# Taking the last head's K pass out of a loop and loading its second half in smaller pieces, in a one-core attention-decode kernel

## Chip, cores, metric

One Trainium2 chip, one of its cores. The metric is device time in microseconds (us) of one execution. The kernel before took 1300.07 us (median of 4 executions, 1299.55 to 1300.87). The profile is of a further execution, of 1300.63 us; its span, which leaves out start and end, is about 1.8 us shorter than the time.

## The reference

A decode step for one token: layer norm, 32-head attention over a cache of 32,768 positions per head, output projection, residual, layer norm, a small MLP, residual.

```python
h = x + A(layernorm(x))           # x: 1 x 1 x 512, bf16
#   q = (x @ wq) as 32 heads of 128
#   p = softmax(q . k_cache * 128**-0.5)     k_cache: 32 x 32768 x 128 bf16
#   A = (p @ v_cache) as one row @ wo        v_cache: the same shape
out = h + B(layernorm(h))         # 512 -> 1376 -> 512, h * tanh(softplus(h))
```

The two caches are 8 MB per head each, 512 MB in all, read once. Everything else is small.

## The kernel before

PE is the engine for matmuls, DVE the vector engine, ACT the scalar engine; SBUF is the memory on the chip, PSUM the memory that matmuls write. K and V of a head stand in SBUF in one ring of two halves of 8 MB. A head is 32 groups of 8 x 128 positions. For each group PE transposes K (8 matmuls against an identity), DVE copies the result from PSUM, PE forms the scores (8 matmuls), and, 40 groups behind, PE forms the values of the head before (8 matmuls). A load is 4 MB, half a head, and is issued when the half that it overwrites has been used. The last V has no half of its own: it goes where the last K was, as soon as that is transposed.

The plan of the loads (cut):

```python
PIECE = 128
FIRST = [8, 8, 16, 32, 64, 128]          # K of head 0
LAST = [128, 64, 32, 16, 8, 8]           # V of head 31
LAG = 8
...
for h in range(H):
    for kind in "kv":
        own = h == 0 if kind == "k" else h == H - 1
        sizes = (FIRST if kind == "k" else LAST) if own else [PIECE] * NH      # NH = 2
        ...
        if kind == "k":
            after = [f"trb{(h - 1) * GH + g1 - 1}"] if h else []     # K: after the same groups of the K before
        else:
            after = [f"pv{(h - 1) * GH + g1 - 1}"] if h else ...     # V: after the values of the V before
            if own:
                after = [f"trb{h * GH + g1 - 1}"]                    # V 31: after the transposes of K 31
```

128 in such a list is 4 MB in rows of 32 KB per partition; 64 has 16 KB rows, 32 has 8 KB rows, and so on.

Only PE's program has a loop. DVE, ACT and the queue of loads are straight code; PE runs heads 2 to 31 as 30 rounds of one body:

```python
for hk in range(2):
    for t in range(GH):
        group(hk, t)

S.repeat(range(2, H), whole)              # whole(hk): the 32 groups of head hk

for t in range(GH):                       # after the last K: values alone
    group(H, t)                           # t = 1: maximum of the last scores, t = 3, 4: to all partitions, exp
    if t == 1:
        y_init()
        for h in range(H - 2, H):
            w_bar(h)                      # row sums on DVE
        ...
    if 2 <= t <= LAG:
        ... y_cols(h) ...                 # 4 "column products" per head, 30 heads: wo times the head's output
```

After that come the column products of the last head, a layer norm, the MLP and the store.

Of the kernel before, what the change touches and what calls it, by code (L numbers as in the profile page):

```python
# [13 lines left out]
PE, ACT, DVE, POOL, SP = "pe", "act", "dve", "pool", "sp"  # L14


PIECE = 128
FIRST = [8, 8, 16, 32, 64, 128]
LAST = [128, 64, 32, 16, 8, 8]

LAG = 8

# [138 lines left out]
def plan_loads(H, GH):  # L161


    NH = GH * 8 // PIECE
    loads = []
    for h in range(H):
        for kind in "kv":
            own = h == 0 if kind == "k" else h == H - 1
            sizes = (FIRST if kind == "k" else LAST) if own else [PIECE] * NH
            assert sum(sizes) == GH * 8 and max(sizes) <= PIECE  # L170
            g = 0
            for j, n in enumerate(sizes):
                g1 = g + n // 8
                if kind == "k":
                    after = [f"trb{(h - 1) * GH + g1 - 1}"] if h else []
                    pos, count = h * GH + g, h
                else:
                    after = [f"pv{(h - 1) * GH + g1 - 1}"] if h else ["q_done"] if g1 > GH // 2 else []
                    if own:
                        after = [f"trb{h * GH + g1 - 1}"]  # L180
                    pos, count = (h + 1) * GH + LAG + g + 0.5, h + 1
                chan = f"{kind}own{j}" if own else f"{kind}{j}"
                loads.append(_Load(kind, h, g, g1, pos, chan, 16 if own else 16 * count, after))
                g = g1
    loads.sort(key=lambda x: x.pos)
    return loads


def build_kernel(nc, A_x, A_k_cache, A_v_cache, A_wq, A_wo, B_w1, B_b1, B_w2, out, NE=4):
# [3 lines left out]
    H = HD // Dh  # L193
# [5 lines left out]
    GH = Sk // (128 * R)  # L199
    NCOL = GH * R  # L200
    NK = H * GH
    FJ = (F + 127) // 128
# [28 lines left out]
    identb = sb([128, 128], BF16, "identb")  # L231
# [25 lines left out]
    FP = FJ + FJ % 2  # L257
    b1r = sb([FP, 128], BF16, "b1r")
    b1T = sb([128, FJ], F32, "b1T")
# [8 lines left out]
    hlp = ps([128, 512], "hlp")  # L268
    yps = ps([128, 512], "yps")
    T_b = [ps([128, R * 128], f"tps{i}", BF16) for i in range(2)]  # L270
# [3 lines left out]
    M_REG = hlp[:, 132:132 + KC]  # L274
    V_REG = hlp[:, 140:141]
    Q0 = 160
    YC = yps[:, 0:KC * WIDE:WIDE]
    HROW = 128
    YM = yps[:, 256:257]
# [32 lines left out]
    def program(S):  # L312
        t_ = nc.tensor
        a = nc.scalar
        v = nc.vector
# [4 lines left out]
        def issue(ld):  # L320
            cache = A_k_cache if ld.kind == "k" else A_v_cache

            part, n = divmod(ld.g0 * R, PIECE)
            src = cache[0, ld.h, part * PIECE * 128:(part + 1) * PIECE * 128, :].rearrange(
# [27 lines left out]
        for _, ld in sorted(order, key=lambda o: o[0]):  # L352
            if isinstance(ld, str):
                load_weights(ld)
            else:
                issue(ld)
        S.dma(SP, lambda: sp.dma_start(out[0, 0, :].rearrange("(g n) -> g n", g=4), outsb[0:128:32, :]).then_inc(sems["out"], 16),
              waits=["fin"])
# [29 lines left out]
               name="ident", waits=["iota"])  # L388
# [20 lines left out]
        def transposes(i):  # L409
            ld = kload.get(i)  # L410
            tb = T_b[i % 2]
            hk, t = i // GH, i % GH
            waits, take = ["identb"] if hk == 0 else [], {}
            if ld:
                waits.append((ld.chan, ld.count))
                if hk:
                    take[1] = (ld.chan, 16)
            if hk >= 2 and t in (GH // 4, 3 * GH // 4):
                half = 1 if t == GH // 4 else 0
                take[2] = (f"{DVE}{half}{PRIV}", DVE_ROUND[half])  # L420
            if hk >= 2 and t == GH // 2 + 4:
                take[3] = (ACT + PRIV, 2)
            if i >= 2:
                waits.append(f"ev{i - 2}")
            for r in range(R):
                S.step(PE, lambda r=r: t_.matmul(  # L426
                    tb[:, r * 128:(r + 1) * 128], block("k", i, r), identb[:, :],
                    is_transpose=True, start=True, stop=True),
                    name=(f"trb{i}" if r == R - 1 else None), waits=(waits if r == 0 else ()), take=take.get(r))
# [22 lines left out]
        def values(i):  # L452
            h, g = divmod(i, GH)
            ld = vload.get(i)
            ob = o_b[0 if g < GH - LAG else 1]
            waits, take = [], {}
            if g == 0:
                waits.append(f"exp{h}")
            if g == GH - LAG:
                waits.append(f"exq{h}")  # L460
            if ld:
                waits.append((ld.chan, ld.count))
                if h < H - 1:
                    take[1] = (ld.chan, 16)
            for r in range(R):
                c = g * R + r
                S.step(PE, lambda r=r, c=c: t_.matmul(  # L467
                    ob[:, 0:WIDE], block("v", i, r), pbuf[:, c:c + 1].to_broadcast([128, WIDE]),
                    start=(r == 0 and g in (0, GH - LAG)), stop=(r == R - 1 and g in (GH - LAG - 1, GH - 1))),
                    name=(f"pv{i}" if r == R - 1 else None), waits=(waits if r == 0 else ()), take=take.get(r))  # L470

        def y_cols(h):
            waits = [f"oT{h}", ("wo", 16)]
            for c in range(KC):
                S.step(PE, lambda c=c: t_.matmul(  # L475
                    yps[:, c * WIDE:(c + 1) * WIDE], wo_sb[:, h, c * 128:(c + 1) * 128],
                    oT[:, h:h + 1].to_broadcast([128, WIDE]),
                    start=False, stop=(h == H - 1), skip_group_check=True), waits=(waits if c == 0 else ()),
                    name=(f"yc{h}" if c == KC - 1 else None))
# [12 lines left out]
        def group(hk, t):  # L492
# [49 lines left out]
            if 0 <= iv < NK:  # L542
                values(iv)
# [15 lines left out]
        def w_bar(h):  # L559
            S.step(DVE, lambda: v.tensor_reduce(wbar[:, h:h + 1], wo_sb[:, h, :], AXX, ALU.add), waits=[("wo", 16)],  # L560
                   name=f"wbar{h}")
# [6 lines left out]
            for t in range(GH):  # L568
                group(hk, t)

        S.repeat(range(2, H), whole)


        hl = H - 1
        for t in range(GH):
            group(H, t)
            if t == 1:
                y_init()
                for h in range(H - 2, H):
                    w_bar(h)  # L580
                S.step(DVE, lambda: v.tensor_scalar_mul(wbh[:, 0:1], wbar[:, hl:hl + 1], 1.0 / D), name="wbh0",
                       waits=[f"wbar{hl}"])
                S.step(DVE, lambda: v.scalar_tensor_tensor(
                    wbh[:, 1:2], wbar[:, hl:hl + 1], 1.0 / D, wbh[:, 0:1], ALU.mult, ALU.subtract), name="wbh",
                    waits=["wbh0"])
            if 2 <= t <= LAG:
                for h in range((H - 2) * (t - 2) // (LAG - 1), (H - 2) * (t - 1) // (LAG - 1)):
                    y_cols(h)
            if t == LAG + 2:
                y_cols(H - 2)  # L590
                S.step(DVE, lambda: v.tensor_tensor(wbo[:, 0:hl], wbar[:, 0:hl], oT[:, 0:hl], ALU.mult), name="wbo",
                       waits=[f"yc{H - 2}"])
                S.step(DVE, lambda: v.tensor_reduce(wbs[:, :], wbo[:, 0:hl], AXX, ALU.add), name="wbs", waits=["wbo"])
            if t == LAG + 6:
                S.step(PE, lambda: t_.matmul(YM, onesm[:, :], wbs[:, :], start=False, stop=False, skip_group_check=True),
                       waits=["wbs"])
                S.step(PE, lambda: t_.matmul(T_b[0][:, 0:FP], b1r[:, :], identb[0:FP, 0:FP],
                                             is_transpose=True, start=True, stop=True),
                       name="b1t", waits=[("b1", 32), f"ev{NK - 2}", f"ev{NK - 1}"])
                S.step(DVE, lambda: v.tensor_copy(b1T[:, :], T_b[0][:, 0:FJ]), name="b1T", waits=["b1t"])  # L600
        for t in range(LAG):
            group(H + 1, t)

# [3 lines left out]
        for s in range(2):  # L607
            S.step(PE, lambda s=s: t_.matmul(
                YM, wbh[:, s:s + 1].to_broadcast([128, 128]), oT[:, hl:hl + 1],
                start=False, stop=(s == 1), skip_group_check=True),  # L610
                waits=(["wbh"] if s == 0 else ()), name=("ym" if s == 1 else None))
        S.step(DVE, lambda: v.tensor_scalar(HC, YC, YM, MEANX, ALU.subtract, ALU.subtract),
               name="hc", waits=["ym"])
# [4 lines left out]
        for j in range(FJ):  # L618
            W = 128 if j < FJ - 1 else FLAST
            for kc in range(KC):  # L620
                S.step(PE, lambda j=j, W=W, kc=kc: t_.matmul(  # L621
                    pre[0:W, j:j + 1], w1v[:, kc, j * 128:j * 128 + W], xcT[:, kc:kc + 1],
                    start=(kc == 0), stop=(kc == KC - 1)),
                    name=("hid" if j == FJ - 1 and kc == KC - 1 else None),
                    waits=(["xcT", ("w1", 16), f"exq{H - 1}"] if j == 0 and kc == 0 else ()))
            if j == FJ // 2:
                S.step(PE, lambda: t_.matmul(V_REG, onesm[:, :], SSQ2, start=True, stop=True), name="v2",
                       waits=["ssq2"])
        S.step(ACT, lambda: a.activation(LNV2, V_REG, ACTF.Ln, bias=EPSC), name="ln2", waits=["v2"])
        S.step(ACT, lambda: a.activation(RSTD2, LNV2, ACTF.Exp, scale=-0.5), name="rstd2", waits=["ln2"])  # L630
        for c in range(KC):
            S.step(PE, lambda c=c: t_.matmul(
                yps[32 * c:32 * c + 1, HROW:HROW + 128], hcol[:, c:c + 1], ident[:, :],
                start=False, stop=False, skip_group_check=True), waits=(["hcol"] if c == 0 else ()))
        z, zm, e, u, uz, den, rden = (hs[:, k, :] for k in range(7))
        S.step(DVE, lambda: v.scalar_tensor_tensor(z, pre[:, 0:FJ], RSTD2, b1T[:, :], ALU.mult, ALU.add),
               name="z", waits=["hid", "rstd2", "b1T"])
# [7 lines left out]
        for j in range(FJ):  # L645
            W = 128 if j < FJ - 1 else FLAST
            waits = ["act", ("w2", 32)] if j == 0 else ()
            for c in range(KC):
                S.step(PE, lambda j=j, W=W, c=c: t_.matmul(  # L649
                    yps[32 * c:32 * c + 1, HROW:HROW + 128], actT[0:W, j:j + 1], w2v[0:W, j, c * 128:(c + 1) * 128],  # L650
                    start=False, stop=(j == FJ - 1), skip_group_check=True),
                    name=("y2" if j == FJ - 1 and c == KC - 1 else None), waits=(waits if c == 0 else ()))
# [46 lines left out]
```

## Time and profile before

| stage | us from the span's start | read from |
|---|---|---|
| first half of K 31 lands, PE starts it | 1238.9 | chain of waits |
| PE has done its 16 groups | 1255.5 | timeline |
| second half of K 31 lands, PE starts it | 1259.3 | timeline |
| PE leaves the loop | 1275.1 | timeline |
| exp of the last scores | 1279.4 | timeline |
| last values done | 1290.6 | chain |
| end of span | 1298.8 | page |

First the page: DMA busy in tenths and GB/s in 40 slices of the span, and the DMA queues with number of packets, MB and share.

```profile
span 1298.8 us, 52290 instructions
...
DMA  9999999999999999999999999999999999999994
GB/s 375 423 411 409 431 430 431 434 433 430 429 434 433 430 430 433 430 432 432 433 429 432 433 431 431 431 434 429 426 431 429 432 432 429 432 432 430 431 433 184
...
q1 hardware_dynamic: 26840, 548.09, 98.8%
q8 instruction: 21, 0.34, 0.1%
q14 instruction: 13, 0.11, 0.0%
```

The loads run at about 430 GB/s to the last slice, so the body is bound by them. The Trainium skill, "DMA: Bandwidth & Descriptors", "Specifications", gives a fabric ceiling of 435 GB/s; the slices agree. Queues 8 and 14 are not data: they bring the engines' instructions. On queue 8 a packet is 16 KB; on queue 14 one is 8 KB.

Next the timeline of PE around the gap: start, length, engine, line, what it did, and in brackets the idle time before it and what ended it. In the names of the program `tps` are the transposes of K, `sps` the scores, `ops` the values and `yps` the column products.

```profile
1255.13 0.35 PE L467 MATMUL ops<-pbuf,ring 128*128 128x32 bf16 x8
1259.29 1.03 PE L426 MATMUL tps<-identb,ring 128*128 128x128 bf16 x8 [3.81 <-DMA ring<-in_A_k_cache_dram]
...
1260.60 1.01 PE L426 MATMUL tps<-identb,ring 128*128 128x128 bf16 x8
```

PE sits idle for 3.81 us until the second half of K 31 lands. Then eight transposes take 1.0 us instead of 0.6: the clock is at half (the view by windows shows a granted clock of 0.50 from 1260 to 1264). The Trainium skill, "TensorE: Matmul & The Clock Gate", Part 1, says that the clock falls to half after an idle window of about 3.4 us; this gap of 3.8 us agrees.

The chain of waits that ended last, from the end of the loop on (start, length, what):

```profile
1276.86 1.20 DVE wbar L560 x2
...
1278.56 0.20 DVE gmax L517
...
1279.18 0.30 PE ops L467 x8
1279.48 0.40 PE yps L475 x16
...
1285.32 5.30 PE ops L467 x200
...
1290.65 0.23 DVE oT L555
```

PE, not a load, holds the end: the values of V 31 run as 200 matmuls without a break until 1290.6. The two row sums (`wbar`, 1.20 us) stand between the maximum per partition and the maximum of all.

Last, the completions of each load. A load has one for each of the sixteen DMA engines (the Trainium skill, "DMA: Bandwidth & Descriptors", "Why a DMA increments its semaphore by 16 and not by 1", says that they finish independently; the trace's records of the landing semaphores agree). From these records, in us:

| load | first | second to last | last |
|---|---|---|---|
| K 31, second half | 1250.77 | 1253.96 | 1259.25 |
| V 30, second half | 1260.60 | 1263.66 | 1268.96 |
| V 31, first half | 1270.31 | 1273.40 | 1278.70 |
| V 31, last piece | 1280.46 | 1283.25 | 1288.56 |

In these loads one completion is always 5.3 us late (at 772 us it was 0.6 us; it grew in five steps of about 0.95); the records do not name its engine, but the constant lag points to one. PE arrives at the last group of V 31 at about 1290.4. So the loads are only 1.9 us behind PE as a limit.

### The profile page before, as it was taken

What the parts mean: (1) busy time and instruction counts of PE and PEld (TensorE: products, weight loads), DVE (VectorE), ACT (ScalarE), POOL (GpSimd) and SP (SyncE); (2) the same over time, 40 slices, a digit from 0 to 9 for tenths busy, and PEclk for the clock granted to TensorE, in tenths of its full rate; (3) what the DMA queues carried; (4) which work ended last, traced back from release to release, by engine and by line L of the source; (5) the groups of instructions that cost most, each with busy time, mean ns of one, the idle gap of its engine ahead of it and who ended that gap; (6) DMA issues with size and microseconds to landing.
All of it is one profiled execution on the core that took longest, in us unless ns stands there. A gap on an engine that the chain in (4) does not pass through costs nothing.

```text
span 1298.8 us, 52290 instructions
## 1 busy us (share of the span) xinstructions
PE 1028.0 (79%) x25199; PEld 997.0 (77%) x25199; DVE 775.3 (60%) x1377; ACT 34.0 (3%) x134; POOL 2.5 (0%) x10
## 2 busy tenths in 40 slices
PE   6757777877877888877877877977877887877878
PEld 6757777877877877877877877877877877777877
DVE  5635555655665656665655665655656656655654
ACT  0000000000000000000000000000000000000000
POOL 0000000000000000000000000000000000000000
PEclk8869888999888989889999889888889989989988
DMA  9999999999999999999999999999999999999994
GB/s 375 423 411 409 431 430 431 434 433 430 429 434 433 430 430 433 430 432 432 433 429 432 433 431 431 431 434 429 426 431 429 432 432 429 432 432 430 431 433 184
DMA packets 26970, 548.54 MB, mean 422 GB/s; under 512 B 2520, under 2 KB 8504, under 8 KB 10296
## 3 DMA queue, kind: packets, MB, share of 16 engines
q1 hardware_dynamic: 26840, 548.09, 98.8%
q8 instruction: 21, 0.34, 0.1%
q14 instruction: 13, 0.11, 0.0%
q0 software_dynamic: 96, 0.00, 0.0%
HBM read 548.08 MB, written 0.00 MB: 422 GB/s over the span
## 4 chain that ended last, share of the span: by engine, by line
DMA 60%; PE 35%; DVE 3%; issue 1%; SPq 0%; ACT 0%
DMA ring<-in_A_k_cache_dram 51%; PE tps L426 18%; DMA ring<-in_A_v_cache_dram 10%; PE ops L467 8%; PE sps L447 7%; DVE kt L435 1%; PE hlp L531 1%; DVE scb L513 1%; PE hlp L515 1%; DVE pmax L511 1%; PE hlp L519 1%; PE yps L475 0%; SPq L328 0%; PE yps L649 0%; PE sps L621 0%
## 5 line engine op out<-in xcount | busy, mean ns | idle before, releaser
L435 DVE COPY kt<-tps 128x1024 bf16<-128x1024 bf16 x1024 | 707.6, 691 | 495.4 <-PE tps L426 488.5
L426 PE MATMUL tps<-identb,ring 128*128 128x128 bf16 x8192 | 696.8, 234 | 193.4 <-DMA ring<-in_A_k_cache_dram 192.2
L426 PEld LDWEIGHTS tps<-identb,ring 128*128 128x128 bf16 x8192 | 524.1, 104 | 200.5 <-DMA ring<-in_A_k_cache_dram 198.6
L467 PE MATMUL ops<-pbuf,ring 128*128 128x32 bf16 x8192 | 361.5, 178 | 55.5 <-DMA ring<-in_A_v_cache_dram 53.9
L447 PE MATMUL sps<-qcur,kt 128*128 128x32 bf16 x8192 | 376.3, 180 | 10.3 <-DVE scb L513 7.4
L447 PEld LDWEIGHTS sps<-qcur,kt 128*128 128x128 bf16 x8192 | 329.0, 99 | 18.3 <-DVE scb L513 14.9
L467 PEld LDWEIGHTS ops<-pbuf,ring 128*128 128x128 bf16 x8192 | 281.6, 97 | 68.3 <-DMA ring<-in_A_v_cache_dram 54.2
L522 ACT ACTIVATE pbuf<-scb,nbias 128x192 bf16<-128x192 f32 x32 | 14.6, 455 | 1183.4 <-PE ops L467 1105.8
L560 DVE TENSOR_REDUCE wbar<-wo_sb 128x1 f32<-128x512 bf16 x32 | 21.5, 676 | 0.0
L531 PE MATMUL hlp<-esum,onesf 128*128 128x1 f32 x128 | 19.1, 253 | 0.0
L531 PEld LDWEIGHTS hlp<-esum,onesf 128*128 128x128 f32 x128 | 17.1, 194 | 0.0
L511 DVE TENSOR_REDUCE pmax<-sps 128x1 f32<-128x256 f32 x32 | 13.3, 415 | 0.5 <-PE sps L447 0.5
L515 PE MATMUL hlp<-ident,pmax 128*1 128x128 f32 x64 | 13.4, 294 | 0.0
L513 DVE COPY scb<-sps 128x256 f32<-128x256 f32 x32 | 13.3, 415 | 0.0
L526 ACT ACTIVATE pbuf<-scb,nbias 128x64 bf16<-128x64 f32 x32 | 11.1, 348 | 61.5 <-PE ops L467 61.5
L519 PE MATMUL hlp<-gmax,onesr 1*128 1x1 f32 x64 | 12.1, 256 | 0.6 <-DVE gmax L517 0.6
L519 PEld LDWEIGHTS hlp<-gmax,onesr 1*128 1x128 f32 x64 | 9.4, 182 | 1.8 <-DVE gmax L517 0.7
L555 DVE SCALAR_TENSOR_TENSOR oT<-ops,rtot,o1s 128x1 bf16<-128x1 f32 x32 | 6.8, 212 | 3.4 <-PE ops L467 3.4
L547 DVE TENSOR_SCALAR o1s<-ops,rtot 128x1 f32<-128x1 f32 x32 | 6.7, 209 | 3.5 <-PE ops L467 3.5
L517 DVE TENSOR_REDUCE gmax<-hlp 1x1 f32<-1x128 f32 x32 | 8.7, 271 | 0.1
L526 ACT ACTIVATION_READ_ACCUMULATOR pbuf<-scb,nbias 128x1 f32 x32 | 6.0, 187 | 0.0
L522 ACT ACTIVATION_READ_ACCUMULATOR pbuf<-scb,nbias 128x1 f32 x32 | 6.0, 186 | 0.0
(80 smaller groups left out, 60.2 us busy)
## 6 DMA issues: line engine op xcount, KB each, us to landing
ring<-in_A_k_cache_dram SPq DMA_DIRECT2D x63, 4096.0 KB, 23.1
ring<-in_A_v_cache_dram SPq DMA_DIRECT2D x63, 4096.0 KB, 20.9
wo_sb<-in_A_wo_dram SPq DMA_DIRECT2D x1, 4096.0 KB, 38.8
ring<-in_A_wq_dram SPq DMA_DIRECT2D x1, 3584.0 KB, 31.2
ring<-in_A_k_cache_dram SPq DMA_DIRECT2D x1, 2048.0 KB, 13.8
ring<-in_A_v_cache_dram SPq DMA_DIRECT2D x1, 2048.0 KB, 15.9
w_sb<-in_B_w_dram SPq DMA_DIRECT2D x1, 1376.0 KB, 24.7
w_sb<-in_B_w_dram SPq DMA_DIRECT2D x1, 1280.0 KB, 25.6
```

The costliest lines, as they stand in the source:

```text
L426: S.step(PE, lambda r=r: t_.matmul(tb[:, r * 128:(r + 1) * 128], block("k", i, r), identb[:, :], is_transpose=True, start=True, stop=True) ...
L435: dve(i, lambda: v.tensor_copy(kt[:, i % NE, :], T_b[i % 2][:, :]), f"ev{i}", waits)
L447: S.step(PE, lambda r=r, c=c: t_.matmul(S_b[:, c:c + WIDE], kt[:, i % NE, r * 128:(r + 1) * 128], q.to_broadcast([128, WIDE]), start=True, ...
L467: S.step(PE, lambda r=r, c=c: t_.matmul(ob[:, 0:WIDE], block("v", i, r), pbuf[:, c:c + 1].to_broadcast([128, WIDE]), start=(r == 0 and g i ...
L511: dve(i, lambda: v.tensor_reduce(pmax[:, :], S_b[:, 0:NCOL], AXX, ALU.max), f"pmax{hs}", [f"qkb{hs * GH + GH - 1}"])
L513: dve(i, lambda: v.tensor_copy(scb[:, :], S_b[:, 0:NCOL]), f"sc{hs}", [])
L515: S.step(PE, lambda: t_.matmul(A_REG, pmax[:, :], ident[:, :], start=True, stop=True), name=f"A{hs}", waits=[f"pmax{hs}"] + (["qT" if H > ...
L519: S.step(PE, lambda: t_.matmul(B_REG, onesr[0:1, :], gmax[0:1, :], start=True, stop=True), name=f"B{hs}", waits=[f"gmax{hs}"])
L522: S.step(ACT, lambda: a.activation(pbuf[:, 0:CV], scb[:, 0:CV], ACTF.Exp, bias=nb[:, :], scale=SC, accum_out=esum[:, 0:1]), name=f"exp{hs} ...
L526: S.step(ACT, lambda: a.activation(pbuf[:, CV:NCOL], scb[:, CV:NCOL], ACTF.Exp, bias=nb[:, :], scale=SC, accum_out=esum[:, 1:2]), name=f"e ...
L531: S.step(PE, lambda s=s: t_.matmul(C_REG, onesf[:, :], esum[:, s:s + 1], start=(s == 0), stop=(s == 1)), name=(f"C{hs}" if s else None), w ...
L560: S.step(DVE, lambda: v.tensor_reduce(wbar[:, h:h + 1], wo_sb[:, h, :], AXX, ALU.add), waits=[("wo", 16)], name=f"wbar{h}")
```

## The change

Its intent: PE shall not wait for the second half of the last K. That half comes in four 1 MB pieces, and so does the second half of V 30, which is then needed earlier. Since the loop's rounds must all wait on the same things, the last head is taken out of the loop. Being straight code, it can also take the column products and the row sums, which then no longer stand between the last scores and the last values. The diff (cut):

```diff
-FIRST = [8, 8, 16, 32, 64, 128]
-LAST = [128, 64, 32, 16, 8, 8]
+FIRST_K = [8, 8, 16, 32, 64, 128]
+LAST_K = [128, 32, 32, 32, 32]
+LAST_V = {2: [128, 32, 32, 32, 32], 1: [128, 64, 32, 16, 8, 8]}
 ...
-        S.repeat(range(2, H), whole)
+        S.repeat(range(2, H - 1), whole)
 
         hl = H - 1
         for t in range(GH):
-            group(H, t)
-            if t == 1:
+            group(hl, t)
+            if t == LAG + 1:
                 y_init()
                 for h in range(H - 2, H):
                     w_bar(h)
+            if LAG + 2 <= t < GH - 6:
+                k, span = t - LAG - 2, GH - 8 - LAG
+                for h in range((H - 2) * k // span, (H - 2) * (k + 1) // span):
+                    y_cols(h)
 ...
-            if 2 <= t <= LAG:
-                for h in range((H - 2) * (t - 2) // (LAG - 1), (H - 2) * (t - 1) // (LAG - 1)):
-                    y_cols(h)
+        for t in range(GH):
+            group(H, t)
```

(Left out: names of semaphores, which loads the loop resets, and the transpose of b1, which moves along.)

More of the change, by code (lines that the diff above doesn't have):

```diff
@@ L167, in plan_loads @@
         for kind in "kv":
-            own = h == 0 if kind == "k" else h == H - 1
-            sizes = (FIRST if kind == "k" else LAST) if own else [PIECE] * NH
+            sizes = [PIECE] * NH
+            if kind == "k":
+                sizes = FIRST_K if h == 0 else LAST_K if h == H - 1 else sizes
+            else:
+                sizes = LAST_V.get(H - h, sizes)
+            own = len(sizes) > NH
             assert sum(sizes) == GH * 8 and max(sizes) <= PIECE
@@ L178, in plan_loads @@
                     after = [f"pv{(h - 1) * GH + g1 - 1}"] if h else ["q_done"] if g1 > GH // 2 else []
-                    if own:
+                    if h == H - 1:
                         after = [f"trb{h * GH + g1 - 1}"]
                     pos, count = (h + 1) * GH + LAG + g + 0.5, h + 1
-                chan = f"{kind}own{j}" if own else f"{kind}{j}"
+                chan = f"{kind}{h}_{j}" if own else f"{kind}{j}"
                 loads.append(_Load(kind, h, g, g1, pos, chan, 16 if own else 16 * count, after))
@@ L276, in build_kernel @@
     Q0 = 160
+    BT = 200
     YC = yps[:, 0:KC * WIDE:WIDE]
@@ L415, in transposes @@
                 waits.append((ld.chan, ld.count))
-                if hk:
+                if 0 < hk < H - 1:
                     take[1] = (ld.chan, 16)
@@ L462, in values @@
                 waits.append((ld.chan, ld.count))
-                if h < H - 1:
+                if h < H - 2:
                     take[1] = (ld.chan, 16)
@@ L580, in program @@
                     w_bar(h)
+            if LAG + 2 <= t < GH - 6:
+                k, span = t - LAG - 2, GH - 8 - LAG
+                for h in range((H - 2) * k // span, (H - 2) * (k + 1) // span):
+                    y_cols(h)
+            if t == GH - 4:
+                S.step(PE, lambda: t_.matmul(hlp[:, BT:BT + FP], b1r[:, :], identb[0:FP, 0:FP],
+                                             start=True, stop=True), name="b1t", waits=[("b1", 32)])
+                S.step(DVE, lambda: v.tensor_copy(b1T[:, :], hlp[:, BT:BT + FJ]), name="b1T", waits=["b1t"])
                 S.step(DVE, lambda: v.tensor_scalar_mul(wbh[:, 0:1], wbar[:, hl:hl + 1], 1.0 / D), name="wbh0",
@@ L596, in program @@
                        waits=["wbs"])
-                S.step(PE, lambda: t_.matmul(T_b[0][:, 0:FP], b1r[:, :], identb[0:FP, 0:FP],
-                                             is_transpose=True, start=True, stop=True),
-                       name="b1t", waits=[("b1", 32), f"ev{NK - 2}", f"ev{NK - 1}"])
-                S.step(DVE, lambda: v.tensor_copy(b1T[:, :], T_b[0][:, 0:FJ]), name="b1T", waits=["b1t"])
         for t in range(LAG):
```

## The prediction

> **What bounds it now.** The page's slices show the DMA engines busy to the last slice at 430 GB/s: loads bound the body, and the change leaves their bytes alone. Only the end can gain. There the chain of waits and the timeline run: the second half of the last K lands (transposes start at 1259.3 us, after PE idled 3.9 us for it), 16 groups of transposes, scores and values until 1275.1, softmax (exp at 1279.4), V 31's values until 1290.6 with column products between them, the MLP, end at 1298.8. From 1259.3 to 1290.6 PE was the limit, partly at half clock: four groups took 1.29 us instead of 0.85 after the idle time.
>
> **But the loads are close behind.** Each load has sixteen completions, one per DMA engine, which finish independently (the Trainium skill, "DMA: Bandwidth & Descriptors", "Why a DMA increments its semaphore by 16 and not by 1"; the trace's landing records agree). At the end fifteen engines are done by 1280.5 to 1283.3 us, but one is last each time: V 31's first half lands at 1278.7, its other pieces at 1283.6, 1286.0, 1287.3, 1287.9, 1288.6. That engine has long been saturated (9.71 us per 4 MB load). It fell behind by some 0.95 us about every 118 us, where 8 KB instruction packets appear (779, 898, 1015, 1135, 1254 us).
>
> **What the change does.**
> - The last K's second half comes in four 1 MB pieces: at 2.43 us per MB the first lands near 1251 to 1252, so PE, which finishes the first half's groups near 1255, no longer waits. This removes 4 us of idle time and 1.8 us of half clock.
> - V 30's pieces are needed earlier too; estimates 1259, 1264, 1266.5, 1269, each before PE's need.
> - 120 column products (about 3 us: 0.40 us per 16) and two row sums (1.3 us of DVE) move into that body. They lengthen it, but no longer sit between last scores and exp, where the sums held the maximum by about 1 us.
> - PE should finish the last K's groups near 1272 to 1273, exp at 1275.5 to 1277, 3 us earlier.
> - Then PE waits for V 31's first half until 1278.7, and afterwards piece by piece. The values end about 0.25 us after the last landing: 1288.8 instead of 1290.6. The gain is 1.8 us, not 6. The tail stays 8.2 us, perhaps 0.3 more at half clock after the new idle time.
> - About 1,800 more PE instructions are outside the loop: estimated 7 more 16 KB instruction packets (the Trainium skill, "Runtime: NRT & Kernel Launch", "Instruction fetch mechanics": 256 instructions per block; the trace's packet sizes agree). In the prologue they slowed eight other engines by 1.7 us each, not this one: no cost expected. Unrolled groups there ran at 0.85 us: no fetch stall either.
>
> **Prediction.** 1300.5 - 1.8 + 0.3 = 1299.0 us, 8 in 10 between 1297.2 and 1300.7. Faster by over 2%: 1%; within 2%: 98%; slower: 1%.
>
> **What would show it.** No gap near 1255, groups of the last K at 0.85 to 1.05 us, exp 3 us earlier, a new PE wait of 1.5 to 3 us on the V cache just before V 31's values, and a chain that ends through V loads. V 31's last landing within 1 us of 1288.6.
>
> **What would make it wrong.** Instruction packets that hit the last engine (+1.7 us each); smaller pieces that let that engine catch up, making the gain 3 us; a PE stall where the loop is left; row sums that delay evictions by more than the 2 us of slack.

## The result

The kernel after took 1303.41 us (median of 4, 1301.71 to 1303.78) beside 1300.07 before. The ratio is 1.0023, 95% interval 1.0005 to 1.0040. A ratio here is the mean time of one kernel's fast runs over that of the other's of the same rounds, so not quite the ratio of the medians. By the 2% rule it is the same; but it is 3.3 us slower by the medians, where I had forecast 1.5 us faster, and lies outside my range.

The page of the kernel after:

```profile
span 1302.0 us, 52297 instructions
...
DMA  9999999999999999999999999999999999999994
GB/s 378 422 414 410 427 432 433 432 431 430 432 434 432 430 432 428 434 434 432 433 425 434 434 430 433 428 433 432 432 428 421 434 429 433 430 430 430 431 422 158
...
q8 instruction: 27, 0.44, 0.1%
```

The bytes of data are the same. Queue 8 has 27 packets instead of 21: six more blocks of PE's instructions.

The timeline of PE, the same columns, at three places in the last K's groups:

```profile
1255.33 0.25 PE L482 MATMUL yps<-oT,wo_sb 128*128 128x32 bf16 x4
1256.72 0.27 PE L482 MATMUL yps<-oT,wo_sb 128*128 128x32 bf16 x4 [1.13 <-issue]
...
1260.82 0.23 PE L482 MATMUL yps<-oT,wo_sb 128*128 128x32 bf16 x3
1262.94 0.28 PE L482 MATMUL yps<-oT,wo_sb 128*128 128x32 bf16 x5 [1.90 <-issue]
...
1266.96 0.33 PE L482 MATMUL yps<-oT,wo_sb 128*128 128x32 bf16 x7
1269.45 0.19 PE L482 MATMUL yps<-oT,wo_sb 128*128 128x32 bf16 x1 [2.16 <-issue]
```

Before each gap PE is in the middle of a run of eight column products: 4 of them, a gap, the other 4; 3 and 5; 7 and 1. Nothing that the profile records ends the gap, so it says "issue". A head has four products, and the program waits only before the first of them; after 3 or 7 of 8 there is no wait in the program at all.

The waits of PE from 1235 us on in the kernel after (us in total, times, longest):

```profile
PE yps L482 <- issue: 6.6, 4, 2.2
PE tps L433 <- DMA ring<-in_A_k_cache_dram: 3.4, 1, 3.4
...
PE tps L433 <- issue: 0.9, 1, 0.9
```

The same view of the kernel before:

```profile
PE tps L426 <- DMA ring<-in_A_k_cache_dram: 7.2, 2, 3.8
...
PE ops L467 <- DMA ring<-in_A_v_cache_dram: 0.4, 1, 0.4
```

The wait that the change was to take away is gone: 7.2 us for K in two waits became 3.4 us in one. In its place are 7.5 us of "issue" in five. The chain of waits of the kernel after, as above:

```profile
1255.58 1.13 issue
...
1261.05 1.90 issue
...
1267.29 2.16 issue
...
1278.56 0.89 issue
...
1284.45 1.45 issue
...
1288.29 5.28 PE ops L474 x200
1293.59 0.23 DVE oT L562
```

The trace's records of packets show what these gaps have in common. Each ends 1.2 to 1.6 us after a 16 KB packet of queue 8 has ended:

| packet starts | packet ends | PE's gap |
|---|---|---|
| 1254.40 | 1255.49 | 1255.58 to 1256.72 |
| 1260.49 | 1261.51 | 1261.05 to 1262.94 |
| 1266.85 | 1267.87 | 1267.29 to 1269.45 |
| 1277.06 | 1277.99 | 1278.56 to 1279.45 |
| 1283.56 | 1284.50 | 1284.45 to 1285.90 |

In before there are four such packets after the loop, and no "issue" wait over 0.5 us beside them. The Trainium skill, "Runtime: NRT & Kernel Launch", "Instruction fetch mechanics", says that an engine's instructions come in blocks of 16 KB, 256 instructions. The packets of queue 8 agree; those of queue 14, which e6 below shows to be DVE's, are of 8 KB. A group with column products is 32 matmuls, each with its weight load: 64 instructions. Four such groups are a block, and indeed the first three gaps lie four groups apart. One group between the second and the third gap has four products instead of eight, 8 instructions fewer, which fits the shift from 3 to 7 products before the gap. (The packet after them started early, at 1270.76, and left no gap.)

Exp came at 1283.0 instead of 1279.4, the last values ended at 1293.6 instead of 1290.6.

Such gaps could have been seen before the change was made. The waits of PE over the whole of before list them:

```profile
PE sps L447 <- issue: 2.9, 2, 2.1
...
PE hlp L399 <- issue: 2.6, 1, 2.6
...
PE ops L467 <- issue: 1.2, 1, 1.2
```

In its timeline these are one gap of 2.59 us that ends at 44.67, at the end of head 0, and gaps of 0.79, 2.07 and 1.17 us that end at 110.52, 117.54 and 124.38, in the first round of the loop. Each ends 1.35 to 1.5 us after a packet of queue 8 has ended (43.31, 109.03, 116.19 and 122.99). Between 185 us, in the second round, and 1280 us queue 8 brings nothing, and the rounds show no such gap.

### The profile page after: what moved, and what is told of

Read it like the earlier page. It is cut to its first block, busy times and chain, and to the rows that moved or that the text cites. A ratio compares the mean times of both kernels' runs of the same rounds, so it can differ in the third digit from the quotient of the medians.

```text
span 1302.0 us, 52297 instructions
## 1 busy us (share of the span) xinstructions
PE 1030.6 (79%) x25199; PEld 999.0 (77%) x25199; DVE 774.7 (59%) x1377; ACT 34.0 (3%) x134; POOL 2.5 (0%) x10
## 4 chain that ended last, share of the span: by engine, by line
DMA 58%; PE 37%; DVE 3%; issue 1%; SPq 0%; ACT 0%
DMA ring<-in_A_k_cache_dram 55%; PE tps L433 19%; PE ops L474 8%; PE sps L454 7%; DMA ring<-in_A_v_cache_dram 3%; DVE kt L442 1%; PE hlp L538 1%; DVE scb L520 1%; PE hlp L522 1%; DVE pmax L518 1%; PE hlp L526 1%; PE yps L482 0%; SPq L335 0%; PE sps L631 0%; PE yps L659 0%
## 5 line engine op out<-in xcount | busy, mean ns | idle before, releaser
L482 PE MATMUL yps<-oT,wo_sb 128*128 128x32 bf16 x128 | 6.4, 177 | 7.0 <-issue 6.6
L482 PEld LDWEIGHTS yps<-oT,wo_sb 128*128 128x128 bf16 x128 | 4.8, 96 | 7.4 <-issue 7.0
```

The lines of the kernel that those rows point to most:

```text
L482: S.step(PE, lambda c=c: t_.matmul(yps[:, c * WIDE:(c + 1) * WIDE], wo_sb[:, h, c * 128:(c + 1) * 128], oT[:, h:h + 1].to_broadcast([128, ...
```

## The experiments

My theory, T1: outside the loop PE is starved of instructions, because the packets that bring them queue behind loads. Rivals: T2, that it is the column products and row sums, put where PE is the limit; T3, that the 8 KB rows load slower.

### e1: only the loop

```diff
-        S.repeat(range(2, H), whole)
+        S.repeat(range(2, H - 1), whole)
+        whole(H - 1)
```

(to the kernel before, with the resets of semaphores in the last head left out)

> The kernel before with the last K's groups merely taken out of the loop: old pieces, old place of the column products, the same work. Theory T1 (PE is starved of instructions: outside the loop each 256 instructions come as one 16 KB packet through the loaded DMA engines, about 6.2 us apart, while 256 instructions of groups are only 4.5 us of work): 6 more 16 KB instruction packets than before, 2 to 4 stalls of 1 to 2 us each that the profile calls issue in the last K's groups, one of them possibly hidden in the 4 us wait for the last K's second half; time 2 to 5 us over before. Rival T2 (the slowdown is the 3 us of column products and the row sums put into a body that PE limits; where the instructions come from doesn't matter): the same as before within 0.5 us, no stalls.

Measured: 1303.17 us beside 1300.38 (5 and 9 runs), ratio 1.0023 [1.0009, 1.0036]. 27 packets on queue 8. The waits of PE in the last K's groups:

```profile
PE tps L426 <- issue: 2.5, 2, 1.7
PE ops L467 <- DMA ring<-in_A_v_cache_dram: 2.1, 1, 2.1
...
PE tps L426 <- DMA ring<-in_A_k_cache_dram: 0.9, 1, 0.9
```

Two gaps of 1.68 and 0.85 us by "issue"; the wait for K is down to 0.9 us, because one gap lies in it. With the same work, the same pieces and the same order, taking 32 groups out of the loop costs 2.8 us, nearly as much as the whole change (3.3). The profile is of the fastest of the five runs, 1302.33 us; in it the last values came 1.7 us later than in before, and 1.4 of that are the gaps of 0.85 us and of 0.53 (between exp and the last values). T1 holds; T2 and T3 expected nothing here.

### e2: the column products back

```diff
-            if LAG + 2 <= t < GH - 6:
-                ... y_cols(h) ...
 ...
+            if 2 <= t <= LAG:
+                ... y_cols(h) ...          # after the body, as before
```

(to the kernel after)

> The change with only the 120 column products back after the body. T1: the total of instructions outside the loop is the same, so the stalls stay, now one for every 5.3 groups instead of 4: 3 or 4 of 1 to 2 us in the last K's groups; time within 1.5 us of the change, over 1301. T2: the body is 3 us shorter, no stall of over 0.3 us, time 1300.3 or less. A third idea, T3 (the 8 KB pieces load slower and that is the loss) expects the time of the change, without stalls.

Measured: 1303.16 us beside 1300.38, ratio 1.0018 [1.0005, 1.0032]. The gaps are there without column products in the body, 1.43, 1.83, 1.64 and 1.49 us in the last K's groups and one of 1.71 later; exp came at 1280.5, 2.6 us earlier than in the change, but the products and the last gap then stood between exp and the last values, which ended at 1293.1 instead of 1293.6. So T2 is right that the products lengthen the body, and wrong that this is the loss: it expected 1300.3 us or less, and moved back, they give next to nothing.

### e3: pieces in the loop, for all heads

```diff
+MID = [128, 64, 64]
...
-            sizes = (FIRST if kind == "k" else LAST) if own else [PIECE] * NH
+            sizes = (FIRST if kind == "k" else LAST) if own else MID
```

(to the kernel before)

> The kernel before, all of the last K in the loop, but every head's second half in two 2 MB pieces (16 KB rows, which loaded at 4.87 us, the full rate). T1: no instruction packets or stalls before the column products, PE goes through 1255 us without the 4 us wait, exp 3 to 4 us earlier than before (near 1275 to 1276), then it waits for V 31; the end is bound by the last landing near 1288.6: 1298.0 to 1299.5 us. T3 (pieces cost more than they give): 1301 or more, at a loading rate under that of before.

Measured: 1304.58 us beside 1300.38, ratio 1.0032 [1.0018, 1.0046]. A miss: I expected 1298.0 to 1299.5. Exp came at 1280.3, and V 31 landed at 1294.4 instead of 1288.6. Two things that I had not costed: the landings of a 2 MB piece are 4.89 to 4.90 us apart, where half of a 4 MB load is 4.86, and 62 halves of heads pay that twice (an estimate from these numbers: 62 x 0.07 us, 4 to 5 us); and the sorting by position put a piece of V 29 behind K 31's first half, so PE waited 4.2 us for it. The first is T3's idea, on all heads; but e3 has more loads as well as shorter rows, and no run tells these two apart. In the change only two halves have small rows: eight 1 MB pieces landed 2.45 to 2.51 us apart, 2.49 typically, against 2.43 (a quarter of 9.71); one came 3.39 us after the piece before it, with an 8 KB packet of queue 14 between them (at 1253.96). Estimate: 8 x 0.06, 0.5 us, and not on the way of PE, which was late by more than that.

### e4: the instruction stream without the loads

```diff
+    loads = [x for x in loads if not (x.g0 >= GH // 2 and (x.kind, x.h) in (("k", H - 1), ("v", H - 2))
+                                      or (x.kind, x.h) == ("v", H - 1))]
     loads.sort(key=lambda x: x.pos)
```

(to the kernel after; it computes with old bytes, which the tolerance did not notice, and nobody waits for what isn't loaded)

> The change without the loads of the second halves of the last K and of V 30 and of all of V 31 (wrong result on purpose; the old bytes are used): the DMA engines are empty from about 1249 us on, the instruction stream is the same. If the stalls are instruction packets held up behind loads (T1a): packets come at most 4.2 us apart, stalls in the last K's groups under 0.4 us each, groups with column products 1.05 us throughout. If a packet's latency is the same without loads (T1b): the same four stalls of 0.9 to 2.2 us. If the stalls come from the column products' own waits (T2b): the same stalls as well, but not at block borders.

Measured: one run of 1294.64 us (state unknown), profiled. The page still has 27 packets on queue 8, and these are all of PE's waits that the view lists from 1235 us on, but for two of 1.1 and 0.6 us in the MLP:

```profile
PE tps L435 <- DMA ring<-in_A_k_cache_dram: 3.4, 1, 3.4
...
PE yps L484 <- DVE oT L564: 0.3, 1, 0.3
PE sps L456 <- DVE scb L522: 0.2, 1, 0.2
```

Its timeline of PE, where the change had its first gap:

```profile
1255.27 0.35 PE L484 MATMUL yps<-oT,wo_sb 128*128 128x32 bf16 x8
1255.47 0.61 PE L435 MATMUL tps<-identb,ring 128*128 128x128 bf16 x8
```

No "issue" at all: where the change broke off after 4 of 8 products at 1255.58, here all 8 run and the next group follows. Groups with column products take 1.05 us throughout. The packets start 3.8 to 5.2 us apart in the last K's groups, at PE's own pace, instead of 5.9 to 6.4 us. (I had expected at most 4.2.) Up to the 14th group of the last K, PE is at the same place in both runs within 0.1 us. Yet the first two packets start at 1246.08 and 1251.25 here, and at 1248.52 and 1254.40 in the change: 2.4 and 3.2 us later. Once they move, these two take 0.9 us here and 1.0 to 1.1 there, so nearly all of the delay lies before the packet starts to move.

The last group's K is copied at 1273.0 and exp comes at 1276.0, where the prediction had 1272 to 1273 and 1275.5 to 1277; in the change these came at 1279.8 and 1283.0. Of these 6.8 us the four gaps before are 6.1. So the gaps are not a price of straight code as such, nor of the column products: they appear when the packets come beside the loads. This is the run that decides for T1: PE lacks its instructions because the loads make the packets late.

### e5: half of the last head in the loop

```diff
+        for t in range(GH // 2):
+            group(2, t)
         def whole(hk):
-            for t in range(GH):
+            for t in range(GH // 2, GH):
                 group(hk, t)
+            for t in range(GH // 2):
+                group(hk + 1, t)
         S.repeat(range(2, H - 1), whole)
         ...
-        for t in range(GH):
+        for t in range(GH // 2, GH):
             group(hl, t)
```

(to e2; the loop is turned by half a head, the start of the column products and the row sums move to the 19th group, the names of some semaphores change)

> The pieces of the change, but the loop turned by half a head (second half of one K, first half of the next), so that only the second half of the last K is outside it; column products after it, as before. The runs so far showed that about 10 groups after the loop come without a stall, their instructions being there already. T1 (instruction packets held up behind loads): 3 packets fewer than the change; PE goes through 1255 us without a wait of over 0.5 us and stalls once or twice, 1 to 2 us each, from the 26th group on; exp at 1275 to 1278 us, 5 us earlier than in the change; then a wait for V 31; the values end within 0.5 us of the last landing, near 1289 to 1290; time 1298.5 to 1300.3. If the loss is in the pieces or in the loop's exit and not in the number of instructions outside: 1302 or more.

Measured: 1300.84 us (1299.78 to 1301.60) beside 1299.97, ratio 1.0005 [0.9991, 1.0018]. Seven packets after the loop instead of ten (the total stays 27, since half of head 2 now stands before the loop). No wait near 1255; gaps of 0.85 us at 1264.5, 1.52 at 1270.3, 1.64 at 1276.7 and 0.49 at 1282.6; exp at 1276.1; last values at 1289.7. The mechanism came as expected; the median is 0.5 us over my range. The profile cannot say why: it is of the fastest of the five runs, 1299.78 us, which lies in the range, and the five fall into two at 1299.8 to 1299.9 and three at 1300.8 to 1301.6. Besides the gaps that I had allowed for in the last K's groups, it shows one of 1.64 us just after exp.

### e6: more DVE instructions

```diff
+            if 2 <= hk < H and t in (10, 12, 14, 18, 20, 22):
+                for _ in range(2):
+                    S.step(DVE, lambda: v.memset(scr[:, n:n + 1], 0.0), count=False)
```

(to the kernel before; `n` is a new column each time)

> The kernel before with 12 needless one-column memsets per head on DVE (about 350 instructions in all). My claim of the prediction that the last DMA engine fell behind through DVE's instruction packets: 2 or 3 more 8 KB packets, each putting the last completion 0.95 us further behind the one before it, so a last landing of V 31 near 1290.5 to 1291.5 instead of 1288.6, and 0.5 to 2 us more time. If that engine is late for another reason: the last landing stays within 0.6 us of 1288.6.

Measured: 1303.92 us (4 runs) beside 1299.97, ratio 1.0028 [1.0013, 1.0044]. The page:

```profile
q8 instruction: 21, 0.34, 0.1%
q14 instruction: 16, 0.13, 0.0%
```

Three more 8 KB packets on queue 14, and V 31's last landing at 1291.9 instead of 1288.6, 3.3 us later. In the landing records of e6 the last completion slips by 0.94 to 1.01 us at the load after each of eight such packets from 540 us on, as it did by 0.92 to 0.97 us after five of them in before. So the late DMA engine is late because of DVE's instruction packets, about 1.1 us for each of the three; the slips stand at the packets, so it is these and not DVE's further work. This part of the prediction holds. Its sizes were too small: I expected the landing at 1290.5 to 1291.5, and 0.5 to 2 us more time where there were 3.95; the 0.6 us that the time lost beyond the landing are not traced.

### e8: only the row sums moved

```diff
+                if hk == H - 1 and t in (LAG + 3, GH // 2 + 1):
+                    w_bar(H - 2 if t == LAG + 3 else H - 1)
 ...
-                for h in range(H - 2, H):
-                    w_bar(h)
```

(to the kernel before; DVE alone is touched: two small steps that use the sums move to a later group)

> The kernel before with only the two row sums of wbar moved off the way from last scores to exp, into the last K's groups (nothing on PE changes, all of it stays in the loop). If PE's chain from last scores to last values bound the end, as I read before's profile: the maximum is taken about 1 us earlier, exp near 1278.4, time 0.6 to 1.1 us less, and not below 1298.4, which the last landing allows. If the loads bound the end already: no change.

Measured: 1300.00 us beside 1299.97, ratio 0.9997 [0.9983, 1.0011]. A miss. From the maximum per partition to that of all it was 1.39 us instead of 2.37, so the sums did hold it; exp was 0.4 us earlier (1278.98), and yet the last values ended at 1290.64, where they had at 1290.65. PE's waits show where it went:

```profile
PE ops L467 <- issue: 0.9, 2, 0.7
```

Two gaps of 0.68 and 0.20 us now stand between exp and the last values, and each ends about 1.45 us after a packet of queue 8. (PE had also started the second half of K 31 0.28 us later in this profile.) So the end of the kernel before was already close to what the packets allow, not only to what PE's work allows. This is read from one profile, of the slowest of the five runs.

### e9: the pieces with all of the last head in the loop

The loop's rounds must wait alike. Here the loop waits, at the two further pieces of K, on two more semaphores, which are raised once at the start by what the 29 looped heads before the last take off; for the last head only its loads raise them. No PE code outside the loop changes.

```diff
+PARTS = [128, 64, 32, 32]          # K 31 and V 30
 ...
+            elif 2 <= hk < H - 1 and t in (24, 28):
+                waits.append((f"kx{2 if t == 24 else 3}", 16 * (hk - 1)))
+                take[1] = (f"kx{2 if t == 24 else 3}", 16)
 ...
+        for j in (2, 3):
+            S.dma(POOL, lambda j=j: g_.memset(fill[:, j - 2:j - 1], 0.0).then_inc(sems[f"kx{j}"], 16 * (H - 3)))
```

(to the kernel before)

> The kernel before with the whole last K inside the loop and still its second half (2, 1 and 1 MB) and that of V 30 in pieces: the loop waits on two more semaphores, which for the other heads are filled once at the start. All PE code outside the loop is as before. If the pieces are worth what I predicted and the change lost it to instruction packets (T1): 4 packets after the loop, no stall before the loop's end, no 4 us wait near 1255 us, last K's groups done near 1269 to 1270, exp at 1273 to 1275.5; the end is held by V 31's last landing (1288.6 to 1289) or by packets of the tail: 1298.3 to 1299.8 us. If the pieces have nothing to give even so (the loads hold the end, or the tail's own packets do): 1300.0 to 1301.

Measured: 1299.71 us (1299.62 to 1300.35) beside 1300.45, ratio 0.9996 [0.9982, 1.0009]: as fast as before, and the five runs lie wholly under the four of the change (1301.71 and more, taken in other rounds). Most of what I had predicted for the change is in its profile. PE goes through 1255, as its timeline shows:

```profile
1255.05 0.35 PE L479 MATMUL ops<-pbuf,ring 128*128 128x32 bf16 x8
1255.25 0.61 PE L438 MATMUL tps<-identb,ring 128*128 128x128 bf16 x8
```

and then waits for V 31. Its waits:

```profile
PE ops L479 <- DMA ring<-in_A_v_cache_dram: 4.0, 3, 3.5
PE tps L438 <- DMA ring<-in_A_k_cache_dram: 3.4, 1, 3.4
```

Its chain of waits, from the loop's end on:

```profile
1268.65 20.19 DMA ring<-in_A_v_cache_dram
...
1288.89 0.38 PE ops L479 x8
...
1289.29 0.23 DVE oT L567
```

The K waits are 3.4 us as in the change, but no "issue" is among the waits. The longest wait for V, 3.5 us, is over the predicted 1.5 to 3: here the column products were not moved ahead of exp, which came earlier than predicted. Exp came at 1273.1, 6.3 us earlier than before. V 31's last piece landed at 1288.85, and the last values were done at 1289.29, 1.36 us earlier than before. By the medians it gained 0.7 us, which the interval doesn't separate from nothing.

### e10: e9 with the row sums of e8

```diff
+                if hk == H - 1 and t in (LAG + 3, GH // 2 + 1):
+                    w_bar(H - 2 if t == LAG + 3 else H - 1)
 ...
-                for h in range(H - 2, H):
-                    w_bar(h)
```

(to e9)

> The same with the two row sums moved into the last K's groups as in the earlier run. If V 31's last landing or the tail's packets hold the end by now, the same time as the run beside it within 0.5 us; if PE's way from last scores to exp still did, 0.4 to 1 us less.

Measured: 1299.84 us beside 1300.45, ratio 0.9994 [0.9980, 1.0008], the same as e9. PE's longest wait for V 31 grew from 3.5 to 4.2 us; the last piece landed at 1289.3, and the last values were done at 1289.8. Now the last landing holds the end, and no gain shows from a shorter way of PE to exp.

All together (us; "gaps" are PE's "issue" gaps of over 0.5 us from the last K on):

| kernel | packets after the loop | gaps | exp | V 31 landed | last values | ratio to before |
|---|---|---|---|---|---|---|
| before | 4 | 0 | 1279.4 | 1288.6 | 1290.6 | 1 |
| after | 10 | 5 | 1283.0 | 1289.6 | 1293.6 | 1.0023 |
| e1 | 10 | 3 | 1281.1 | 1289.0 | 1292.3 | 1.0023 |
| e2 | 10 | 5 | 1280.5 | 1289.3 | 1293.1 | 1.0018 |
| e5 | 7 | 3 | 1276.1 | 1289.0 | 1289.7 | 1.0005 |
| e9 | 4 | 0 | 1273.1 | 1288.9 | 1289.3 | 0.9996 |

## Why the prediction was wrong

- **What bounds it now.** Right that the loads hold the body and PE the end, and that the last landing, at 1288.6, leaves only 1.8 us to gain. e9 shows this limit, and e6 shows why the last DMA engine is late. Not complete: e8's profile shows that the instruction packets were a third limit close by.
- **No wait for K's second half.** Right: the wait is gone in the change and in e9, and with it the groups at half clock (in the change the granted clock is 1.00 from 1246 to 1270).
- **PE done with the last K near 1272 to 1273, exp at 1275.5 to 1277.** Wrong: its last group came near 1280, exp at 1283.0. Without loads beside the packets (e4) both came as predicted, so the packets' cost is what this sum lacked.
- **The step that failed.** "Unrolled groups there ran at 0.85 us: no fetch stall either" and "no cost expected" of the packets. I counted the packets right (7 more estimated, 6 found), and looked for their cost only in the DMA engines that they slow. The cost was on PE, which waited for what they bring. The evidence from the prologue could not carry the inference: in head 1 the packets come 6.1 to 7.4 us apart, but PE waits for loads so often that it needs a block only about that often; stalls would be hidden in those waits. And just beside the place where I looked, before's trace has four stalls in the open, of 0.79 to 2.59 us, at the end of head 0 and in the first round of the loop (shown above); I overlooked them. The sum that I should have made was of two rates that the trace shows: a block of 256 instructions is 5.3 groups of 48, 4.5 us of work at 0.85 us each (or four groups of 1.05 us, 4.2 us, with column products), and the change's packets start 5.9 to 6.4 us apart where PE waits for them. By this estimate 1.4 to 2.2 us are lost for each block, and the last head is about seven blocks (some 1,800 instructions of PE by the code), of which the first ones are there when the loop ends. Measured: 7.5 us of gaps in place of the 3.8 us of waiting, the groups at half clock and the row sums that the change took away.
- **Then PE waits for V 31.** Wrong for the change: PE was so late that V 31's pieces were there first (the chain has no V load in it after the loop). Right in e9.
- **What would make it wrong.** I named "a PE stall where the loop is left". It was the right place but the wrong kind: not one stall at the exit, but one for every block after it.

What stays open: which part of a packet's delay is spent where. The records show when a packet starts to move, not when PE asked for it; against e4 the delay lies before that start, but whether it is a queue at the DMA engines or the memory behind them was not separated. Also open is how much is brought in advance: the first gap comes ten to fifteen groups after the exit (ten in e5, fifteen in e1), which fits two to three blocks, but this was not tried by itself.

## What to carry to other kernels

Code taken out of a loop has to be brought to the engine, through the same DMA engines as the data (in before a packet of queue 8 at 183.4 us made one of the sixteen completions of a load 1.7 us later). In a kernel that keeps these full, compare for each block of instructions the time of its work with the spacing of the instruction packets in the trace, and do that in a place where the engine doesn't wait for data anyway. Here the first round of the loop was such a place: it had "issue" gaps that end just after a packet. If only one round differs in its waits, let all rounds wait and raise the semaphores beforehand for those that needn't, rather than take the round out.

## What the Trainium skill lacked or had wrong

- "Runtime: NRT & Kernel Launch", "Instruction fetch mechanics", calls the cost of crossing a 16 KB boundary "mostly hidden". With the DMA engines full, five boundaries cost PE 0.89 to 2.16 us each (after); with them empty, nothing (e4). The page also counts the fetch after a taken branch as a reason to prefer full unrolling; here the loop's rounds took nothing from queue 8 between 185 and 1280 us (before), and one unrolled head cost 2.8 us (e1).
- No page says that instruction packets make a DMA engine late with its data, by more with each packet while the loads keep it full: three more 8 KB packets for DVE moved the last landing by 3.3 us (e6). "DMA: Bandwidth & Descriptors", "Latency and other measured facts", tells of engines that are usually slower and offers another cause.
- "DMA: Bandwidth & Descriptors", "Specifications", asks for 512 B or more for line rate. Far above that the rate still fell a little here: per MB, loads with 32 KB rows took 2.43 us, with 16 KB rows 2.445 and with 8 KB rows 2.49 (after, e3); over 62 half heads this is an estimated 4 to 5 of the 5.8 us by which e3's last landing moved. Rows and number of loads were not separated.
- The same table has an HBM limit of about 358 GB/s per core, without its condition; the page's section "Bandwidth" says that it is the share of a core when both cores of an HBM load at once. Here one core loaded alone, and the slices of before show 430 GB/s for over a millisecond.
